# Attention with a cache and a parallel MLP, decode: the first load of wq is cut into 16 and 112 rows

## The chip, the cores and the metric

The kernel runs on one core of a Trainium2 chip. The metric is the device time of one execution in microseconds; a kernel's time is the median over its runs. The core has a matrix engine (TensorE, PE in the profile), a vector engine (VectorE, DVE), an activation engine (ScalarE, ACT), a general engine (GpSimd, POOL) and an engine that only issues DMAs and waits (SyncE, SP). 16 DMA engines move data from HBM, the chip's main memory, to SBUF, the on-chip memory of 128 partitions. "PEq", "SPq" and the like in the profile are an engine's sequencer: the instructions that issue, wait and branch.

## The reference

One token passes through a layer norm, and then through attention over a cache and an MLP at the same time; both are added to the input. All is float32.

```python
# D = 512, 32 query heads, 8 key heads, Sk = 65536 cached keys, Dh = 128, Dff = 1792
q = (x @ wq).reshape(B, Sq, Hq, Dh).transpose(0, 2, 1, 3)
scores = einsum("bhqd,bhkd->bhqk", q, repeat(k_cache, 4)) * Dh ** -0.5
o = einsum("bhqk,bhkd->bhqd", softmax(scores), repeat(v_cache, 4))
A = o.reshape(B, Sq, Hq * Dh) @ wo
B = maximum(x @ w1, 0) @ w2
# with xn = layernorm(x):
return x + A(xn, k_cache, v_cache, wq, wo) + B(xn, w1, w2)
```

## The kernel before

The keys and values of all 8 heads are one row of 524,288 positions, taken in 32 chunks of 16,384 (four to a head). A chunk of k fills the tile `kt`, a chunk of v the tile `vt`, each 128 partitions x 16,384 floats, 8.4 MB. `kt` holds wq ahead of the first chunk and wo behind the last; `wt` holds w1 first and w2 at the end.

**Loads.** All big loads are issued by SyncE, in the order in which they are written. The first, line 151, loads the first 4096 columns of wq for all 128 partitions, a row of 16 KB each. It stands ahead of the hand-synchronised section that begins at line 156. Between them SyncE passes a branch, at which the engines meet. In the section follow the other two parts of wq (line 159; `WQ_CUTS` has 4096, 4096 and 8192 columns), w1 (line 160), and then, each behind a wait, k (line 162) and the loop over v and k (lines 163 to 167). A wait for "kfree" or "vfree" holds an issue until the tile's last reader has signalled. A load adds 16 to its semaphore when all of it has landed. The input x is loaded by ScalarE (lines 234 and 235) on its own queue.

**From x to q.** ScalarE, PE, VectorE and GpSimd compute the layer norm. GpSimd's last step is `xn`, line 212. Then it waits for the first part of wq, which counts on the semaphore "ends" (`take` waits for a count and subtracts it), and copies `xn` into `qpad`, line 214, which signals "q". PE waits for "q", and for the second part of wq on "k", and runs 32 matmuls over all of wq (line 313), of which rounds 0 and 1 read the first part, 2 and 3 the second and 4 to 7 the third. VectorE transposes the results (line 366) and holds rounds 4 to 7 back until the third part has landed on "wq2" (`gates` at line 368). Its last transposes signal "kfree", upon which SyncE issues the first chunk of k.

**GpSimd behind that** waits for w1 and does the MLP's first product (lines 217 to 226); PE's part of it runs in passes beside the attention.

**A turn of the loop.** PE computes the scores of a chunk from `kt`, VectorE transposes them and takes their maximum, ScalarE takes the exponentials, PE multiplies them with `vt`, and VectorE adds to the running result. SyncE issues the next k when VectorE and ScalarE are done with `tr` and `kt`, and the next v when PE is done with `vt`.

Of the kernel before, what the change touches and what calls it, by code (L numbers as in the profile page):

```python
# [40 lines left out]
WQ_CUTS = [4096, 4096, 8192]  # L41
WQ_SEMS = ["ends", "k", "wq2"]
# [2 lines left out]
W2_SUM = 12  # L45
W2_ROWS = 10
PASSES = 3


def take(e, sem, n=1):  # L50

    return e.sem_inc(sem, -n).wait_op(sem, n, "sem-ge")  # L52
# [7 lines left out]
def attention_and_mlp_kernel(  # L60
# [12 lines left out]
    sp, pe, dve, act, pool = nc.sync, nc.tensor, nc.vector, nc.scalar, nc.gpsimd  # L73
    scale = float(DH) ** -0.5

    def sbuf(name, *shape):
        return nc.alloc_sbuf_tensor(name, list(shape), F32).ap()
# [3 lines left out]
    def sem(name):  # L81
        if name not in sems:
            sems[name] = nc.alloc_semaphore(name)
        return sems[name]

    def after(ins, name, n=1):

        return ins.wait_op(sem(name), n, "sem-ge")

    kt = sbuf("kt", P, CHUNK)  # L90
# [47 lines left out]
    wq_row = wq[0].rearrange("p a n -> p (a n)")  # L138
# [9 lines left out]

    load = sp.dma_start(kt[:, : WQ_CUTS[0]], wq_row[:, : WQ_CUTS[0]]).then_inc(sem(WQ_SEMS[0]), 16)  # L151
    tc.no_tile_sem_insts.add(load.ins.name)
    tc.add_to_no_dep_group("first", load.ins)
    tc.declare_fence(pool.nop().ins, group="first")
    section = ctx.enter_context(ExitStack())
    inside = section.enter_context(tc.tile_critical(sync_engine=mybir.EngineType.Pool, no_gpsimd_drain=True))  # L156
    for i in range(1, len(WQ_CUTS)):
        cut = slice(wq_at[i], wq_at[i + 1])
        sp.dma_start(kt[:, cut], wq_row[:, cut]).then_inc(sem(WQ_SEMS[i]), 16)  # L159
# [24 lines left out]
    def link(ins):  # L184

        if chain[0]:
            after(ins, "pool", chain[0])
        chain[0] += 1
        return ins.then_inc(sem("pool"), 1)
# [20 lines left out]
    link(pool.tensor_scalar(st[:, 6:7], st[:, 6:7], -0.5, 1.5, op0=ALU.mult, op1=ALU.add))  # L210
    link(pool.tensor_mul(st[:, 7:8], st[:, 5:6], st[:, 6:7]))
    link(pool.tensor_scalar_mul(xn, xc, st[:, 7:8]))
    take(pool, sem("ends"), 16)
    after(pool.tensor_copy(qpad[:, :XA], xn), "pool", chain[0]).then_inc(sem("q"), 1)
    f = DFF_ALL
    w1_of = [wt[:, a * f : (a + 1) * f] for a in range(XA)]
# [54 lines left out]
    with nc.body("turns", valid_engines=[pe.engine]):  # L271
# [3 lines left out]
        with pe.If(t > 1):  # L275
            after(pe.transpose(pma[:GROUP, :P], m, ident), "d2p").then_inc(sem("p2d"), 1)  # L276
            after(pe.matmul(pmb[:, :GROUP], ones[:GROUP, :], dg, start=True, stop=True), "d2p", 2).then_inc(sem("p2d"), 1)  # L277

            with pe.Fori(0, PASSES):
                for c in range(CT):  # L280
# [175 lines left out]
```

## Time and profile before

| What | Value |
|---|---|
| median of 3 runs | 1303.14 us (1303.03 to 1303.14) |
| span of the profiled execution | 1301.3 us |
| HBM read | 560.99 MB |
| mean rate over the span | 431 GB/s |
| PE busy | 774.9 us (60%) |
| mean granted PE clock | 0.755 |

The span runs from the first to the last instruction of one profiled execution, and the times in its rows count from its start. The median is of whole executions and contains 1.8 us more. Rows of DMAs have a queue's name, the tile loaded and its source. A timeline's row holds the start, the time taken, the engine, the line, the operation, and in brackets the idle time before it with what ended that. "DMA to landing" is the time from issue until the load's semaphore has its count.

### The profile page before, as it was taken

The page shows a single profiled execution, that of the slowest core. Times are in us where ns is not written, and L with a number is a line of the kernel's source. Part 1 is how long each engine was busy: PE and PEld are TensorE (multiplying, and loading weights), DVE is VectorE, ACT ScalarE, POOL GpSimd, SP SyncE. Part 2 cuts the span into 40 slices and gives each one's busy share as a digit, 9 for nine tenths or more (in the row PEclk, how much of TensorE's full clock was granted, in tenths as well). Part 3 has the DMA queues.
Part 4 walks back from the last instruction along what each step waited for, and adds up shares of the span by engine and source line. Part 5 has one row for each costly group of instructions (what it writes and reads, how often), then busy time and mean ns, then how long its engine had stood idle before and what let it go on. Part 6 is the DMA issues. An engine that isn't in the chain of part 4 may idle for free.

```text
span 1301.3 us, 13055 instructions
## 1 busy us (share of the span) xinstructions
PE 774.9 (60%) x5474; PEld 231.1 (18%) x5474; DVE 274.8 (21%) x466; ACT 76.2 (6%) x299; POOL 34.8 (3%) x30
## 2 busy tenths in 40 slices
PE   3365674665576456566555566666567466557557
PEld 1111121111121111121111121111112111112112
DVE  2211222211222220222220122221122221122222
ACT  1000000000000000000000000000000000000000
POOL 1900000000000000000000000000000000000000
PEclk9677877776887777786776777677777777777779
DMA  9999999999999999999999999999999999999998
GB/s 403 451 419 451 419 451 419 435 435 419 451 419 451 419 451 419 449 421 423 447 419 451 419 451 419 451 419 435 435 419 451 419 451 419 451 419 443 427 420 370
DMA packets 11236, 561.02 MB, mean 431 GB/s; under 512 B 1505, under 2 KB 1505, under 8 KB 1890
## 3 DMA queue, kind: packets, MB, share of 16 engines
q1 hardware_dynamic: 11088, 561.00, 99.7%
q10 hardware_dynamic: 146, 0.00, 0.0%
q8 instruction: 1, 0.02, 0.0%
q14 instruction: 1, 0.01, 0.0%
HBM read 560.99 MB, written 0.00 MB: 431 GB/s over the span
## 4 chain that ended last, share of the span: by engine, by line
issue 94%; DMA 3%; POOL 2%; SPq 0%; PE 0%; DVE 0%; POOLq 0%
DMA wt<-w 3%; POOL wt L219 1%; POOL wt L224 0%; POOL wt L222 0%; POOL wt L223 0%; SPq L177 0%; SPq L159 0%; PE banks L339 0%; DVE ysb L417 0%; SPq L151 0%; POOL hT L226 0%; SPq L452 0%; POOLq L156 0%
## 5 line engine op out<-in xcount | busy, mean ns | idle before, releaser
L313 PE MATMUL banks<-kt,qpad 128*32 128x512 f32 x2176 | 310.0, 733 | 311.1 <-PEq L52 308.7
L292 PE MATMUL banks<-vt,probs 128*16 128x512 f32 x2048 | 271.3, 690 | 82.1 <-PEq L52 82.1
L366 DVE STREAM_TRANSPOSE tr<-banks 128x1024 f32<-128x1024 f32 x136 | 170.0, 1250 | 471.4 <-PE banks L313 466.8
L313 PEld LDWEIGHTS banks<-kt,qpad 128*32 128x32 f32 x2176 | 84.5, 131 | 509.6 <-issue 496.3
L281 PE MATMUL banks<-wt,ones 128*1 128x448 f32 x768 | 121.3, 786 | 0.0
L292 PEld LDWEIGHTS banks<-vt,probs 128*16 128x16 f32 x2048 | 68.4, 108 | 298.4 <-issue 298.4
L392 DVE COPY o_sb<-banks 128x512 f32<-128x512 f32 x32 | 22.1, 692 | 455.3 <-PE banks L292 455.3
L254 ACT ACTIVATE corr<-diff 128x8 f32<-128x8 f32 x32 | 6.7, 208 | 1179.8 <-ACTq L52 1179.8
L256 ACT ACTIVATE probs<-tr,nb_new 128x128 f32<-128x128 f32 x128 | 65.3, 521 | 0.0
L276 PE MATMUL banks<-ident,m 128*4 128x128 f32 x32 | 9.7, 303 | 78.9 <-DVE m L384 78.9
L302 PE MATMUL banks<-sel,o_sb 128*128 128x4 f32 x256 | 32.8, 252 | 18.7 <-PEq L52 18.7
L302 PEld LDWEIGHTS banks<-sel,o_sb 128*128 128x128 f32 x256 | 31.0, 191 | 20.6 <-issue 20.6
L226 POOL TENSOR_SCALAR hT<-ysum 128x14 f32<-128x14 f32 x1 | 0.3, 257 | 1220.7 <-DVE ysum L404 1220.7
L384 DVE TENSOR_REDUCE m<-tr 128x4 f32<-128x512 f32 x32 | 32.2, 1006 | 2.9
L281 PEld LDWEIGHTS banks<-wt,ones 128*1 128x1 f32 x768 | 20.2, 100 | 58.9 <-issue 58.4
L277 PE MATMUL banks<-dg,ones 4*128 4x4 f32 x64 | 15.4, 309 | 20.0 <-DVE dg L387 20.0
L256 ACT ACTIVATION_READ_ACCUMULATOR probs<-tr,nb_new 128x1 f32 x128 | 24.0, 187 | 0.0
L276 PEld LDWEIGHTS banks<-ident,m 128*4 128x4 f32 x32 | 2.6, 81 | 108.0 <-DVE m L384 108.0
L219 POOL TENSOR_SCALAR wt<-wt,xn 128x1792 f32<-128x1792 f32 x4 | 19.1, 4797 | 16.5 <-DMA wt<-w 16.5
L277 PEld LDWEIGHTS banks<-dg,ones 4*128 4x128 f32 x64 | 12.6, 245 | 27.1 <-DVE dg L387 27.1
L299 PEld LDWEIGHTS banks<-part_sum,ones 128*128 128x128 f32 x64 | 9.5, 188 | 27.2 <-issue 27.2
L395 DVE TENSOR_TENSOR lo_run<-lo_run,banks 128x8 f32<-128x8 f32 x32 | 5.2, 163 | 40.0 <-DVEq L52 40.0
(69 smaller groups left out, 91.1 us busy)
## 6 DMA issues: line engine op xcount, KB each, us to landing
kt<-wq SPq DMA_DIRECT2D x2, 2048.0 KB, 9.3
kt<-wq SPq DMA_DIRECT2D x1, 4096.0 KB, 20.8
kt<-wo SPq DMA_DIRECT2D x1, 4096.0 KB, 15.5
kt<-wo SPq DMA_DIRECT2D x2, 2048.0 KB, 22.2
wt<-w SPq DMA_DIRECT2D x1, 3584.0 KB, 28.9
wt<-w SPq DMA_DIRECT2D x1, 1536.0 KB, 9.5
wt<-w SPq DMA_DIRECT2D x1, 1024.0 KB, 11.7
kt<-k SPq DMA_DIRECT2D x32, 24.1
```

The source lines that it names most:

```text
L219: last = pool.tensor_scalar_mul(w1_of[a], w1_of[a], xn[:, a : a + 1])
L256: last = act.activation(probs[:, :, g], tr[:, :, g], AF.Exp, bias=nb_new[:, g : g + 1], scale=scale, accum_out=part_sum[:, g : g + 1],)
L276: after(pe.transpose(pma[:GROUP, :P], m, ident), "d2p").then_inc(sem("p2d"), 1)
L277: after(pe.matmul(pmb[:, :GROUP], ones[:GROUP, :], dg, start=True, stop=True), "d2p", 2).then_inc(sem("p2d"), 1)
L281: ins = pe.matmul(hrow[32 * c : 32 * c + 1, :], ones[:, :1], hb[:, :, 32 * c : 32 * c + 32], start=True, stop=True,)
L292: last = pe.matmul(acc[c : c + WIDE * GROUP, :], probs[:, b : b + WIDE, :].rearrange("p b g -> p (b g)"), vt[:, b * DH : (b + WIDE) * DH], ...
L299: pe.matmul(lo_new[:, 0, :], ones, part_sum, start=True, stop=True).then_inc(sem("vfree"), 1)
L302: last = pe.matmul(lo_new[:, 1, :], o_sb[:, b, :], sel[:, b, :], start=(b == 0), stop=(b == WIDE - 1),)
L313: last = pe.matmul(pair[s // 2 % 2][32 * c : 32 * c + 32, s % 2 * 512 : s % 2 * 512 + 512], qpad, kb[:, s * 16 : s * 16 + 16, c, :], start ...
L366: ins = after(dve.transpose(tr2[:, s * 1024 : (s + 1) * 1024], pair[s % 2]), "p2d", s + 1)
L384: dve.reduce_max(m, tr.rearrange("p b i -> p i b")[:, :GROUP, :], axis=AX.X).then_inc(sem("d2p"), 1)
L392: after(dve.tensor_copy(o_sb.rearrange("p b d -> p (b d)"), acc), "p2d", 7).then_inc(sem("d2p"), 1)
```

## The change

The first load is cut by partitions. The load that stays at the place of the old one has the partitions 0 to 15 (`FIRST`), one row of 16 KB for each of 16 DMA engines. The other 112 rows are a second load, the first thing that SyncE issues in the section. Both count on "ends", and GpSimd waits there for 32 rather than 16. Line numbers behind the edits grow by one, and by two behind the second load.

```diff
+FIRST = 16
...
-    load = sp.dma_start(kt[:, : WQ_CUTS[0]], wq_row[:, : WQ_CUTS[0]]).then_inc(sem(WQ_SEMS[0]), 16)
+    load = sp.dma_start(kt[:FIRST, : WQ_CUTS[0]], wq_row[:FIRST, : WQ_CUTS[0]]).then_inc(sem(WQ_SEMS[0]), 16)
     tc.no_tile_sem_insts.add(load.ins.name)
     tc.add_to_no_dep_group("first", load.ins)
     tc.declare_fence(pool.nop().ins, group="first")
     section = ctx.enter_context(ExitStack())
     inside = section.enter_context(tc.tile_critical(sync_engine=mybir.EngineType.Pool, no_gpsimd_drain=True))
+    sp.dma_start(kt[FIRST:, : WQ_CUTS[0]], wq_row[FIRST:, : WQ_CUTS[0]]).then_inc(sem(WQ_SEMS[0]), 16)
     for i in range(1, len(WQ_CUTS)):
         cut = slice(wq_at[i], wq_at[i + 1])
         sp.dma_start(kt[:, cut], wq_row[:, cut]).then_inc(sem(WQ_SEMS[i]), 16)
...
-    take(pool, sem("ends"), 16)
+    take(pool, sem("ends"), 32)
     after(pool.tensor_copy(qpad[:, :XA], xn), "pool", chain[0]).then_inc(sem("q"), 1)
```

On SyncE, at the program's start, the order before is this (`kt<-wq` is the load of wq, the numbers behind it are partitions x floats; `wt<-w` is w1):

```order
L452 UNCONDITIONAL_BRANCH
L151 DMA kt<-wq 128x4096
L452 UNCONDITIONAL_BRANCH
L159 DMA kt<-wq 128x4096
L159 DMA kt<-wq 128x8192
L160 DMA wt<-w 128x7168
L162 DMA kt<-k 128x16384
```

And in the changed kernel:

```order
L454 UNCONDITIONAL_BRANCH
L152 DMA kt<-wq 16x4096
L454 UNCONDITIONAL_BRANCH
L158 DMA kt<-wq 112x4096
L161 DMA kt<-wq 128x4096
L161 DMA kt<-wq 128x8192
L162 DMA wt<-w 128x7168
L164 DMA kt<-k 128x16384
```

One row is new, the load of 112 rows behind the branch. No other engine has another order than before.

## The prediction

> **What bounds the kernel now.** I read the page's queues and slices first, then the run in stretches, then SyncE's issues, then single waits at the start. The page says that one queue's packets fill the 16 DMA engines:
>
> ```profile
> span 1301.3 us, 13055 instructions
> ...
> PE 774.9 (60%) x5474; PEld 231.1 (18%) x5474; DVE 274.8 (21%) x466; ACT 76.2 (6%) x299; POOL 34.8 (3%) x30
> ...
> DMA  9999999999999999999999999999999999999998
> ...
> q1 hardware_dynamic: 11088, 561.00, 99.7%
> ```
>
> No compute engine is over 60%. The stretches (start:end, length, busy time and count per engine, granted clock, mean busy share of the DMA engines, GB/s) say where the rate stands and where it doesn't:
>
> ```profile
> 0.00:1.75 1.75, 0.00 (x0) 0.00 (x0) 0.17 (x1) 0.00 (x0) 0.81 (x9) 1.00 0.00 0
> 1.75:2.40 0.65, 0.00 (x0) 0.00 (x0) 0.29 (x1) 0.44 (x1) 0.49 (x3) 1.00 1.74 403
> 2.40:2.80 0.40, 0.00 (x0) 0.00 (x0) 0.40 (x1) 0.40 (x1) 0.32 (x3) 1.00 0.00 0
> 2.80:3.55 0.75, 0.00 (x0) 0.00 (x0) 0.75 (x1) 0.45 (x1) 0.64 (x5) 1.00 0.90 371
> ...
> 3.50:30.00 26.50, 9.98 (x68) 3.28 (x68) 7.79 (x8) 3.33 (x10) 1.26 (x6) 0.97 1.02 435
> ...
> 70.00:1260.00 1190.00, 722.61 (x5088) 215.58 (x5087) 246.85 (x425) 67.13 (x270) 0.00 (x0) 0.75 1.00 434
> ...
> 1297.00:1301.30 4.30, 1.35 (x38) 0.46 (x28) 0.69 (x2) 0.00 (x0) 0.00 (x0) 1.00 0.09 23
> ```
>
> A packet is put down where it starts, so bytes bunch in short stretches. Nothing moves until 1.75 us. Then 403 GB/s x 0.65 us = 262 KB, which is one row of 16 KB (4096 floats) on each of 16 engines; none starts until 2.80, when the second rows do. From 3.5 us the rate is 435 GB/s and it is still 434 over the 1190 us in the middle: 27.2 GB/s an engine, so a 16 KB row takes 16,384 B / 27.2 GB/s = **0.60 us**. 561 MB at 434 GB/s are 1293 us; with 1.75 us ahead and 4.3 us behind that is 1299 of the 1301.3. The time is one stream, and what shifts its slowest engine shifts the end, as long as loads stay queued. They do:
>
> ```profile
> 0.73 0.39 SPq L151 DMA_DIRECT2D kt<-wq  x1
> 1.34 0.83 SPq L159 DMA_DIRECT2D kt<-wq  x2
> 2.22 0.69 SPq L160 DMA_DIRECT2D wt<-w  x1
> 26.46 0.33 SPq L162 DMA_DIRECT2D kt<-k  x1
> 27.18 0.34 SPq L165 DMA_DIRECT2D vt<-v  x1
> 65.47 0.34 SPq L167 DMA_DIRECT2D kt<-k  x1
> ...
> kt<-wq SPq DMA_DIRECT2D x1, 4096.0 KB, 20.8
> wt<-w SPq DMA_DIRECT2D x1, 3584.0 KB, 28.9
> xT<-x ACTq DMA_DIRECT2D x1, 2.0 KB, 8.2
> ...
> vt<-v SPq DMA_DIRECT2D x1, 42.6
> ```
>
> Columns of the last four: KB and us from issue to landing. The third wq load, issued at about 1.7, lands at 22.5. w1 lands at 2.22 + 28.9 = 31.1 us and the first k load is issued at 26.5, 4.6 us ahead; the first v lands at 27.18 + 42.6 = 69.8 and the second k is issued at 65.5, 4.3 us ahead.
>
> **The change part by part.** It cuts the first DMA (128 rows of 16 KB, 8 to an engine) into 16 rows, issued where the whole was, and 112 rows, issued behind SyncE's branch, ahead of the other wq loads. GpSimd waits for 32 on "ends" in place of 16. Bytes, matmuls and the rest of every engine's order stay.
>
> *One more issue on SyncE.* The L151 row has 0.39 us for one, so the other two wq loads and w1 are issued about 0.4 us later. Their rows are not due until the engines have moved the first 2 MB, 8 x 0.60 = 4.8 us after 1.75; w1's not until all 8.4 MB of wq have gone. Cost 0; without that cover, 0.4 us.
>
> *GpSimd's wait for both parts.* The rows around it:
>
> ```profile
> DMA to landing us min/median/max: 7.2/7.2/7.2
> ...
> 14.15 0.31 POOL L212 TENSOR_SCALAR xn<-xc,st 128x4 f32<-128x4 f32 x1
> 14.52 0.19 POOL L214 COPY qpad<-xn 128x4 f32<-128x4 f32 x1
> ...
> 15.00 5.17 PE L313 MATMUL banks<-kt,qpad 128*32 128x512 f32 x32 [3.03 <-PEq L52]
> ...
> 22.63 3.64 PE L313 MATMUL banks<-kt,qpad 128*32 128x512 f32 x32 [2.46 <-DVEq L368]
> ```
>
> The first row is line 151's: the load lands at 0.73 + 7.2 = 7.9 us. The copy behind the wait starts 0.06 us after the multiply ahead of it, at 14.5, so the wait has 6.5 us to spare. Queued behind it on GpSimd are that copy, which gives PE its q, and then w1's multiplies. Cost 0. If the parts came 6.5 us late or more, q would be late by the rest, but only a lateness beyond 20.2 - 22.6 (the end of PE's first half against the start of its second, which waits for the third wq load through VectorE) would reach the k load.
>
> *An earlier start.* In the stretch 1.75 to 2.40 the 16 first rows start; fine cuts of it put the last start in this one:
>
> ```profile
> 2.28:2.32 0.04, 0.00 (x0) 0.00 (x0) 0.04 (x1) 0.04 (x1) 0.00 (x0) 1.00 0.95 410
> ```
>
> That is 0.04 us x 410 GB/s = one row, 0.55 us behind the first. If a load with an eighth of the rows lets all engines start at 1.75, the slowest gains up to 0.55 us. The second load is issued at 1.34 at the earliest (SyncE's branch ends then), so by the first load's own delays (1.75 - 0.73 = 1.02 to 2.30 - 0.73 = 1.57) its rows are there from 2.36 to 2.91 us, while engines are through with row one from 2.80. The price of its lateness is therefore 0 to 0.1 us now, and all that an earlier first row gains beyond this is waited away again. I take a gain of 0.3, with 0 and 0.55 as ends.
>
> *Rows no longer spread evenly.* Every large load before has 128 rows, so the trace shows 27.2 GB/s on each of 16 lanes, but not what a lane is: an engine, or the group of eight partitions that the engine writes. As long as an engine has partitions of its own the two read alike. Now 16 engines write partitions 0 to 15 together, and then seven rows each of partitions 16 to 127. If a lane is an engine, this costs 0. If a lane is a group of partitions, the first load uses few: with groups that interleave row by row it would use all 16 (cost 0), with blocks of eight neighbours two, so a row takes 8 x 0.60 = 4.8 us; with groups made from runs of four, four lanes, 4 x 0.60 = 2.4 us. I take runs of four, between the ends. Behind it stand 112 rows: the four lanes have 4 rows left, the other twelve all 8, at least 8 x 0.60 = 4.8 us. Together 2.4 + 4.8 = 7.2 us against 4.8 for the load in one: **+2.4 us** with the lanes in perfect use. They won't be: an engine's seven rows run across lane borders, so it queues behind a neighbour in one place and leaves a lane idle in another. I put this at two rows of 0.60, **+1.2 us**, with 0 and four rows (2.4) as ends.
>
> [...]
>
> *Sum:* +2.4 + 1.2 - 0.3 = **+3.3 us** on the slowest engine. It isn't absorbed: k's first issue follows the third wq load (through the second PE half at 22.63) and slides with it, w1's landing slides too, and the 4.6 and 4.3 us of queued work ahead are larger than any unevenness between engines that I allow (four rows, 2.4). Against its own execution: 1301.3 + 3.3 = 1304.6. The median, 1303.14, lies 1.8 us above the span, and I add the same to it: **1306.4 us**. Behind it x also lands later: its 8 packets an engine take turns with wq's rows (issued at 0.98, 8.2 us to landing), so 9.2 becomes 11 to 13 us and the q copy up to 18; PE's first half would end near 24, still ahead of the third wq load at 22.5 + 3.3.
>
> **The rivals.** *Lanes are engines.* Then a row takes 0.60 us wherever it goes and the change is at most a start earlier by 0.55 and at least one late by 0.5 (the new issue's 0.39 and the 0.1): 1302.6 to 1303.6, likeliest 1302.9, not slower. For it speaks that rate and row time are the same for every load; against it that no row in the trace has engines meeting on partitions. It decides if the first rows still take about 1.1 us and the second rows start by 3.5 us.
>
> *Only the first load is hurt.* The seven rows each find free lanes, since early engines pull ahead of late ones and their places spread out: (4 - 1) x 0.60 = +1.8, less 0.3: 1304.6.
>
> *Rows dealt out in turn.* If the second load gives 16 neighbouring rows at a time to the 16 engines, each of its seven rounds is like the first load, 2.4 us: 8 x 2.4 = 19.2 against 4.8, +14.4: 1317.5. The 2 MB would land near 21 us, past the q copy, and k's issue would slide by about as much. Against it: one would have to write seven rounds so, while a block of seven rows per engine is the simpler cut.
>
> *More than 2.6 us faster* asks for more than there is: 1.75 us of empty start, 1.02 of them behind the first issue, and 0.45 us that the first row takes beyond 0.60.
>
> **How the numbers follow.** Lanes by partitions in blocks of seven, 1306.4, own range 1305.8 to 1309.0 (the second term between 0.6 and 2.4, or two lanes in the first load in part): 0.57. Rows in turn: 0.10. Only the first load: 0.11. Lanes are engines: 0.20. Anything faster by more than 0.2%: 0.02. 0.2% is 2.6 us, about what a measurement of this kernel can tell from no change; so slower has 0.57 + 0.10 = 0.67, the same 0.11 + 0.20 = 0.31, faster 0.02. The range from 1302.8 to 1309.0 takes in the forecast, the third case and most of the fourth and leaves the 0.10 at 1317.5 and the lowest part of the fourth.
>
> **What would show it.** In the stretches: first rows that start between 1.75 and 2.0, second rows that start near 4.5 rather than 2.8, and a rate under 435 GB/s up to about 11 us; 435 again from there. k's first issue near 30 in place of 26.46, the last w2 load's end later by as much as that of w1. Wrong, if the second rows start by 3.5 us, if the rate is at 435 by then, or if k's issue slides but the end does not (then the stream has slack that I don't see).

## The result and the profile after

| What | Before | Changed |
|---|---|---|
| median | 1303.14 us (1303.03 to 1303.83, 5 runs) | 1308.79 us (1306.90 to 1312.48, 5 runs) |
| ratio of the means | | 1.0045 (1.0032 to 1.0057) |
| span of the profiled execution | 1301.3 us | 1306.3 us |

The change costs 5.65 us, 0.43%: slower, as forecast, by 1.7 times the +3.3 us of the sum. 1308.79 lies 2.4 us above the forecast of 1306.4 and just inside its range. The runs of the changed kernel also lie 5.6 us apart, those of the kernel before 0.8 us. The page of the changed kernel reads as before but for one instruction and 16 packets more and a longer span; PE is at 59% rather than 60%:

```profile
span 1306.3 us, 13056 instructions
...
q1 hardware_dynamic: 11104, 561.00, 99.7%
```

No average on it shows where 5 us went. The stretches of the changed kernel do (columns as in the prediction: the last three are granted clock, DMA share, GB/s):

```profile
1.75:2.40 0.65, 0.00 (x0) 0.00 (x0) 0.29 (x1) 0.44 (x1) 0.49 (x3) 1.00 1.91 403
2.40:2.80 0.40, 0.00 (x0) 0.00 (x0) 0.40 (x1) 0.40 (x1) 0.32 (x3) 1.00 0.32 42
2.80:3.55 0.75, 0.00 (x0) 0.00 (x0) 0.75 (x1) 0.45 (x1) 0.65 (x5) 1.00 1.89 267
3.55:11.50 7.95, 1.17 (x4) 1.00 (x4) 2.20 (x2) 3.33 (x10) 1.08 (x5) 1.00 0.92 268
11.50:30.00 18.50, 9.76 (x52) 2.51 (x56) 2.59 (x3) 0.00 (x0) 0.19 (x1) 0.86 1.02 437
...
70.00:1260.00 1190.00, 713.62 (x5052) 213.88 (x5052) 242.89 (x422) 68.00 (x274) 0.00 (x0) 0.75 1.00 434
```

And the kernel before in the fourth stretch:

```profile
3.55:11.50 7.95, 0.70 (x3) 0.61 (x3) 2.04 (x1) 1.06 (x6) 0.00 (x0) 1.00 1.01 427
```

The engines count as busy for 92% of that stretch and move 268 GB/s, not 427: they are occupied, but their rows are slow. 159 GB/s less over 7.95 us is 1.26 MB, at 434 GB/s 2.9 us of the stream. From 11.5 us the rate is back. A packet's whole duration is booked where it starts, so the share times the stretch is the mean row where each of 16 engines starts one: 1.91 x 0.65 = 1.24 us for a first row, against 1.74 x 0.65 = 1.13 before. From 2.40 to 3.55 start 42 x 0.40 + 267 x 0.75 = 217 KB, 13 rows, in (0.32 x 0.40 + 1.89 x 0.75) x 16 = 24.7 us of engine time: 1.9 us a row, where one takes 0.60 at full speed. The rows behind the first load suffer more than the first load does.

SyncE's issues in the changed kernel (start, time), and then its loads (KB, us from issue to landing):

```profile
0.73 0.40 SPq L152 DMA_DIRECT2D kt<-wq  x1
1.36 0.32 SPq L158 DMA_DIRECT2D kt<-wq  x1
1.73 0.91 SPq L161 DMA_DIRECT2D kt<-wq  x2
2.69 0.43 SPq L162 DMA_DIRECT2D wt<-w  x1
32.65 0.33 SPq L164 DMA_DIRECT2D kt<-k  x1
```

```profile
kt<-wq SPq DMA_DIRECT2D x1, 4096.0 KB, 23.9
wt<-w SPq DMA_DIRECT2D x1, 3584.0 KB, 31.9
kt<-wq SPq DMA_DIRECT2D x1, 2048.0 KB, 14.7
kt<-wq SPq DMA_DIRECT2D x1, 1792.0 KB, 10.2
kt<-wq SPq DMA_DIRECT2D x1, 256.0 KB, 4.1
xT<-x ACTq DMA_DIRECT2D x1, 2.0 KB, 4.1
```

The first part of wq is complete at 1.36 + 10.2 = 11.6 us rather than 7.9, w1 at 2.69 + 31.9 = 34.6 rather than 31.1: **+3.5 us**; whether that stays to the end is read from further traces below. k's first issue slid further, from 26.46 to 32.65, **+6.2 us**. PE's two halves of the product for q say why:

```profile
16.54 5.96 PE L315 MATMUL banks<-kt,qpad 128*32 128x512 f32 x32 [8.16 <-PEq L53]
26.20 6.25 PE L315 MATMUL banks<-kt,qpad 128*32 128x512 f32 x32 [3.70 <-DVEq L370]
```

The second half starts 3.6 us later, with the third wq load. But it takes 6.25 us rather than 3.64, behind an idle gap of 3.70 us rather than 2.46. Before, w1 landed 4.6 us after k's issue; here 34.6 - 32.65 leaves 1.9 us.

### The profile page after: what moved, and what is told of

It is laid out like the page before. It is cut to its first block, busy times and chain, and to the rows that moved or that the text cites. A ratio compares the mean times of both kernels' runs of the same rounds, so it can differ in the third digit from the quotient of the medians.

```text
span 1306.3 us, 13056 instructions
## 1 busy us (share of the span) xinstructions
PE 772.7 (59%) x5474; PEld 231.0 (18%) x5474; DVE 274.6 (21%) x466; ACT 76.3 (6%) x299; POOL 34.9 (3%) x30
## 4 chain that ended last, share of the span: by engine, by line
issue 93%; DMA 4%; POOL 2%; SPq 0%; PE 0%; DVE 0%; POOLq 0%
DMA wt<-w 4%; POOL wt L221 1%; POOL wt L226 0%; POOL wt L224 0%; POOL wt L225 0%; PE banks L341 0%; SPq L161 0%; SPq L179 0%; DVE ysb L419 0%; SPq L152 0%; PE banks L354 0%; SPq L158 0%; POOL hT L228 0%; SPq L454 0%; POOLq L157 0%
## 5 line engine op out<-in xcount | busy, mean ns | idle before, releaser
L283 PE MATMUL banks<-wt,ones 128*1 128x448 f32 x768 | 117.7, 765 | 0.0
L386 DVE TENSOR_REDUCE m<-tr 128x4 f32<-128x512 f32 x32 | 32.2, 1005 | 2.9
L279 PEld LDWEIGHTS banks<-dg,ones 4*128 4x128 f32 x64 | 11.8, 229 | 27.2 <-DVE dg L389 27.2
L301 PEld LDWEIGHTS banks<-part_sum,ones 128*128 128x128 f32 x64 | 9.5, 188 | 27.2 <-issue 27.2
## 6 DMA issues: line engine op xcount, KB each, us to landing
wt<-w SPq DMA_DIRECT2D x1, 3584.0 KB, 31.9
kt<-wq SPq DMA_DIRECT2D x1, 1792.0 KB, 10.2
```

Source lines behind the costliest of these rows:

```text
L283: ins = pe.matmul(hrow[32 * c : 32 * c + 1, :], ones[:, :1], hb[:, :, 32 * c : 32 * c + 32], start=True, stop=True,)
L301: pe.matmul(lo_new[:, 0, :], ones, part_sum, start=True, stop=True).then_inc(sem("vfree"), 1)
L386: dve.reduce_max(m, tr.rearrange("p b i -> p i b")[:, :GROUP, :], axis=AX.X).then_inc(sem("d2p"), 1)
```

## The experiments

Shortened diffs are against the changed kernel unless said otherwise. "Stream" below is the order of loads that keeps the DMA engines busy; how late it is at a point is read from w1's landing (31.1 us before) and from the issue of y's store (1298.92 us before). A kernel's time is the median of its runs. In the expectations, theory 'late k' is that k's first issue comes so late that the DMA engines run out of queued work.

**Are the lanes engines, or groups of partitions?** Four kernels load the first part of wq in eight loads of 16 rows each. All have the same bytes in the same number of loads; what differs is which 16 partitions are written and which 16 rows of HBM are read. In e6 and e7 the rows of wq stand in another order in the tile, so that their result is not the reference's; the work is the same.

```diff
+    rows = [(slice(16 * i, 16 * i + 16), slice(16 * i, 16 * i + 16)) for i in range(8)]  # e4
+    rows = [(slice(i, P, 8), slice(i, P, 8)) for i in range(8)]                          # e5
+    rows = [(slice(16 * i, 16 * i + 16), slice(i, P, 8)) for i in range(8)]              # e6
+    rows = [(slice(i, P, 8), slice(16 * i, 16 * i + 16)) for i in range(8)]              # e7
...
+    for to, of in rows[1:]:
+        sp.dma_start(kt[to, : WQ_CUTS[0]], wq_row[of, : WQ_CUTS[0]]).then_inc(sem(WQ_SEMS[0]), 16)
...
-    take(pool, sem("ends"), 32)
+    take(pool, sem("ends"), 128)
```

> The first part of wq in eight loads of 16 rows, the rows 16i to 16i+15 of the source into the partitions 16i to 16i+15; each load gives every DMA engine one row. Theory 'partitions' (groups of four neighbours share a lane, so 16 neighbours reach four lanes): rows take up to 2.4 us, the part lands between 14 and 21.5 us, before 7.9. Rival 'source' (what is slow is how the engines read neighbouring rows in HBM): slow too.

> The same eight loads, but load i has every eighth row from i on, in the source and in the partitions. Theory 'partitions' with groups of four: 16 partitions of step eight reach eight lanes, two rows to a lane, rows take 1.2 us, the part lands at 10.5 to 12.5 us. Rival 'source': the rows are apart in HBM, so rows take 0.61 us and it lands near 8.5.

> Strided rows of the source into neighbouring partitions; the rows of wq stand in another order in the tile than in the kernel before. Theory 'partitions': as in the blocks to blocks run, within 1 us. Rival 'source': as in the strided to strided run.

> Neighbouring rows of the source into strided partitions; the rows of wq stand in another order in the tile than in the kernel before. Theory 'partitions': as in the strided to strided run, within 1 us. Rival 'source': as in the blocks to blocks run.

The stretch from 4 to 12 us, in the order e4 (neighbouring partitions from neighbouring rows), e5 (every eighth from every eighth), e6 (neighbouring partitions from every eighth row), e7 (every eighth partition from neighbouring rows):

```profile
4.00:12.00 8.00, 1.17 (x4) 1.00 (x4) 1.75 (x2) 3.33 (x10) 1.08 (x5) 1.00 0.95 117
```
```profile
4.00:12.00 8.00, 1.17 (x4) 1.00 (x4) 1.75 (x2) 3.33 (x10) 1.07 (x5) 1.00 1.04 223
```
```profile
4.00:12.00 8.00, 1.17 (x4) 1.00 (x4) 1.75 (x2) 3.33 (x10) 1.08 (x5) 1.00 1.05 127
```
```profile
4.00:12.00 8.00, 1.17 (x4) 1.00 (x4) 1.75 (x2) 3.33 (x10) 1.07 (x5) 1.00 1.02 213
```

The written partitions decide, the rows read do not: 117 and 127 GB/s into 16 neighbours, 223 and 213 into every eighth partition, with the engines 95% to 105% occupied in all four. A row of 16 KB then takes 0.95 x 16 x 16.4 KB / 117 GB/s = 2.1 us in e4 and, worked out in the same way, 1.2 us in e5. At the prediction's 27.2 GB/s a lane, four lanes are 109 GB/s and eight are 218. Times: 1317.0, 1310.3, 1316.1 and 1309.9 us, one run each, beside 1303.1 before. So how long a row takes depends on the partitions that it is written to. That 16 neighbours have about four of 16 lanes and every eighth partition about eight is an estimate from these rates: 117 and 127 GB/s are 4.3 and 4.7 times 27.2, and 223 and 213 are 8.2 and 7.8 times. No trace shows a lane.

**Is it the cut, or its direction?** The same number of loads, but cut by columns: 512 columns of all 128 rows first, the other 3584 behind the branch (against the kernel before).

```diff
+FIRST = 512
-    load = sp.dma_start(kt[:, : WQ_CUTS[0]], wq_row[:, : WQ_CUTS[0]]).then_inc(sem(WQ_SEMS[0]), 16)
+    load = sp.dma_start(kt[:, :FIRST], wq_row[:, :FIRST]).then_inc(sem(WQ_SEMS[0]), 16)
...
+    sp.dma_start(kt[:, FIRST : WQ_CUTS[0]], wq_row[:, FIRST : WQ_CUTS[0]]).then_inc(sem(WQ_SEMS[0]), 16)
...
-    take(pool, sem("ends"), 16)
+    take(pool, sem("ends"), 32)
```

> The first load keeps the 256 KB but takes them as the first 512 columns of all 128 rows; the other 3584 columns are the second load. Theory 'partitions' (a DMA that writes few partitions is slow, whichever engines carry it): as before, 1302.6 to 1303.6, the rate at 435 GB/s from 3.5 us, the third wq load landing within 0.5 us of before's 22.5. Rival 'small first load' (a second issue behind the branch comes too late, or a small load costs by itself): most of the loss stays, 1306 or more, the third wq load landing past 24.5.

> The kernel with the column cut once more, for a second trace: its runs went from 1304.25 to 1310.45 us although in the traced one the DMA stream ended only 0.1 us later than before and 1.6 us were lost behind it, while the store of y waited to be confirmed. If the spread lies at the end, the last row of w2 ends near 1297.6 again and the whole difference is between the store's issue (1299.0) and its landing. If it lies at the start, the first k row begins later than 30.4 us. If it lies in the loop, the 64 KB rows take more than 2.42 us in some stretch.

e1's stretch, its w1, and its last store (SyncE's issue, then KB and us to landing):

```profile
3.55:11.50 7.95, 1.17 (x4) 1.00 (x4) 2.20 (x2) 3.33 (x10) 1.27 (x6) 1.00 1.01 427
```
```profile
1299.03 0.34 SPq L181 DMA_DIRECT2D y<-ysb  x1
```
```profile
wt<-w SPq DMA_DIRECT2D x1, 3584.0 KB, 28.5
...
y<-ysb SPq DMA_DIRECT2D x1, 2.0 KB, 3.1
```

427 GB/s as before, w1 at 2.69 + 28.5 = 31.2, y's store issued 0.11 us after the 1298.92 of before: cut by columns, the stream loses nothing. Yet e1's time is 1305.48 us (1304.25 to 1310.45, 12 runs), ratio 1.0024 (1.0015 to 1.0033). In its trace the 1.7 us all lie behind the stream: the store of y lands after 3.1 us rather than 1.4. The second trace, e8 (1305.47 us), has the slow store too (2.6 us) and y issued 1.3 us late, with w1 at 31.2 again and k issued at 29.50 rather than 28.27. So the direction of the cut is the cause of the 3.5 us, and it isn't the only thing that the second load costs.

**How much is the 16-row load alone?** Two kernels load the small part into `vt`, which nothing reads before v replaces it, and then all 128 rows into `kt`; once as 16 rows (e14), once as 512 columns (e15), both 262 KB more than before.

```diff
-    load = sp.dma_start(kt[:FIRST, : WQ_CUTS[0]], wq_row[:FIRST, : WQ_CUTS[0]]).then_inc(sem(WQ_SEMS[0]), 16)
+    load = sp.dma_start(vt[:FIRST, : WQ_CUTS[0]], wq_row[:FIRST, : WQ_CUTS[0]]).then_inc(sem(WQ_SEMS[0]), 16)  # e14
+    load = sp.dma_start(vt[:, :512], wq_row[:, :512]).then_inc(sem(WQ_SEMS[0]), 16)                            # e15
...
-    sp.dma_start(kt[FIRST:, : WQ_CUTS[0]], wq_row[FIRST:, : WQ_CUTS[0]]).then_inc(sem(WQ_SEMS[0]), 16)
+    sp.dma_start(kt[:, : WQ_CUTS[0]], wq_row[:, : WQ_CUTS[0]]).then_inc(sem(WQ_SEMS[0]), 16)
```

> The first load takes its 16 rows into the tile of v, where nothing reads them, and the second load takes all 128 rows to their place, so 256 KB more are moved (0.6 us). [...]

> The same with 512 columns of all 128 rows set aside: the same 256 KB more, spread over all partitions. Theory 'partitions': only the 0.6 us of the bytes, the third wq load lands 0.4 to 0.8 us later than before.

w1's issue and its time to landing, in e14 and then in e15:

```profile
2.70 0.44 SPq L162 DMA_DIRECT2D wt<-w  x1
```
```profile
wt<-w SPq DMA_DIRECT2D x1, 3584.0 KB, 30.4
```
```profile
2.68 0.45 SPq L162 DMA_DIRECT2D wt<-w  x1
```
```profile
wt<-w SPq DMA_DIRECT2D x1, 3584.0 KB, 29.1
```

w1 lands at 33.1 and 31.8 us, 2.0 and 0.7 later than before. The 0.7 are the bytes, so the shape of the 16-row load costs 1.3 us. Of the change's 3.5 us the other 2.2 then belong to the 112 rows; that is a difference of single traces, and no run has the 112 rows alone. Times: 1305.26 and 1306.34 us, one run each. e15 has the better stream and the worse time: the second half of PE's product took 6.59 us rather than 3.64, k was issued at 30.12, 1.7 us ahead of w1's landing, and its store of y landed after 3.1 us.

**What does a late k cost?** The kernel before, in which SyncE waits for w1 before it issues the first k:

```diff
     take(sp, sem("kfree"))
+    sp.wait_ge(sem("w1"), 16)
     sp.dma_start(kt, k[0, 0]).then_inc(sem("k"), 16)
```

> The kernel before, in which SyncE waits for w1 to have landed before it issues the first k load, so that the engines run dry once. This prices a dry queue: both theories expect 31.1 + 1.0 us to the first packet, a stop of 1.4 us and slow first rows, 1305 to 1306. If the time goes up by less than 1 us, a late first k cannot be the missing part of the loss; if the runs spread over more than 2 us, a late k alone makes the spread.

1305.94 us (1305.75 to 1306.37, 10 runs), ratio 1.0020 (1.0011 to 1.0029). The first k rows start in this stretch; below it, the same of the kernel before:

```profile
32.20:33.20 1.00, 0.00 (x0) 0.00 (x0) 0.00 (x0) 0.00 (x0) 1.00 (x1) 0.50 3.08 1049
```
```profile
30.30:31.00 0.70, 0.00 (x0) 0.00 (x0) 0.00 (x0) 0.00 (x0) 0.00 (x0) 0.50 3.49 1498
```

1049 GB/s x 1.00 us are 16 rows of 64 KB, 3.08 us each; before, 3.49 x 0.70 = 2.44 us each. They start about 1.9 us later and take 0.64 us longer, together the 2.5 us of the time. In e3 the late issue cost its delay and slow first rows besides.

The two traces of the column cut bear this out. w1 lands at 31.2 us in both; e1 issues k 2.9 us ahead of that, e8 1.7, since PE's second half took 5.34 us in one and 6.57 in the other. Their first k rows, e1 and then e8:

```profile
30.00:30.90 0.90, 0.00 (x0) 0.00 (x0) 0.17 (x1) 0.00 (x0) 0.00 (x0) 1.00 2.72 1165
```
```profile
30.30:31.60 1.30, 0.00 (x0) 0.00 (x0) 0.87 (x3) 0.00 (x0) 0.36 (x1) 1.00 2.28 807
```

Both stretches hold 16 rows, of 2.45 us in e1 and 2.96 in e8, and y is issued 0.1 and 1.3 us later than before. As far as two traces can tell, a k issue 1.8 us later than before (e1) cost nothing, and one 3.0 us later (e8) cost about 1.2 us. No single margin decides: in e10 and e17 below, k is issued 3.0 and 2.9 us ahead of w1's landing, and the first rows take about 3 us.

**The changed kernel with k in time.** Two more executions, without an edit:

> The changed kernel once more, for a second trace: its runs have spans from 1305.1 to 1310.7 us. Theory 'late k': the first 2 MB cost 3.2 to 3.5 us again, and what differs is when the first k load is issued (32.65 in the first trace, later in a slower run) and how slow its first rows are. Rival 'elsewhere': the start is as in the first trace, and the difference lies in the loop or at the store of y.

> The changed kernel, unaltered, a third trace. Theory 'uneven engines behind a late k': if its time is above 1309, the first 64 KB rows of the engines start further apart than the 1.06 us of the first trace, and 64 KB rows of more than 2.5 us are found in the loop. If it is near 1307, they start within 1 us and the loop is free of such rows.

In e9 (1308.12 us) the second PE half took 5.26 us, at a granted clock of 0.50 from 28 to 30 us, and k was issued at 32.38; span 1306.3 again. In e18 (1307.03 us) it took 3.64 us, at a granted clock of 1.00. Its PE, SyncE and stretches:

```profile
16.87 5.76 PE L315 MATMUL banks<-kt,qpad 128*32 128x512 f32 x32 [8.49 <-PEq L53]
26.54 3.64 PE L315 MATMUL banks<-kt,qpad 128*32 128x512 f32 x32 [3.91 <-DVEq L370]
```
```profile
30.37 0.33 SPq L164 DMA_DIRECT2D kt<-k  x1
...
1302.63 0.35 SPq L181 DMA_DIRECT2D y<-ysb  x1
```
```profile
26.00:30.30 4.30, 3.64 (x32) 0.96 (x32) 2.50 (x2) 0.00 (x0) 0.00 (x0) 1.00 0.99 427
...
33.75:34.45 0.70, 0.00 (x0) 0.00 (x0) 0.00 (x0) 0.00 (x0) 0.00 (x0) 1.00 3.47 1498
```

And the profiled execution after the change, where PE was granted half the clock and the first k rows were slow:

```profile
24.70:31.50 6.80, 5.30 (x28) 1.36 (x32) 2.50 (x2) 0.00 (x0) 0.00 (x0) 0.50 0.95 409
33.60:34.30 0.70, 0.00 (x0) 0.00 (x0) 0.60 (x2) 0.00 (x0) 0.00 (x0) 1.00 4.17 1404
```

e18 is close to the forecast: k's issue slid by 3.9 us, the first k rows took 3.47 x 0.70 = 2.43 us as before, y was issued 3.7 us late, the span is 4.0 us longer. In the profiled execution after the change, 1404 GB/s x 0.70 us are 15 rows, and they took 4.17 x 0.70 x 16 / 15 = 3.11 us each, 0.7 more; its y is issued at 1303.94, 5.0 us late. e9 is neither. Its first k rows, and the landing of w1 in e9 and in e18:

```profile
34.10:34.80 0.70, 0.00 (x0) 0.00 (x0) 0.17 (x1) 0.00 (x0) 0.00 (x0) 1.00 3.48 1498
```
```profile
wt<-w SPq DMA_DIRECT2D x1, 3584.0 KB, 32.7
```
```profile
wt<-w SPq DMA_DIRECT2D x1, 3584.0 KB, 32.3
```

In e9 the 16 first rows took 3.48 x 0.70 = 2.44 us: k was issued late, at 32.38, and it cost nothing there. But the loads ahead of k cost more. w1 lands at 2.68 + 32.7 = 35.4 us in e9 and at 2.69 + 32.3 = 35.0 in e18, 4.3 and 3.9 us later than before, where the first trace has 3.5. So one kernel's loads cost 3.5 to 4.3 us. From w1's landing to y's issue the first trace lost another 1.5 us, e9 0.9 (y at 1304.10) and e18 none. The slow first rows account for part of the 1.5; what e9 lost there is not from them and stays open.

The length of PE's gap alone does not say how long the second half takes. Behind gaps of 2.46 us before, 2.14 in e3 and 3.91 in e18 it took 3.64 us; behind gaps of 3.70 in the profiled execution after the change, 4.69 in e9 and 2.05 in e17 below it took 6.25, 5.26 and 5.34. After the change the granted clock was 1.00 until 24.6 us, 2.1 us into the gap, and 0.50 from 24.7 to 31.5; in e9 it was still 1.00 at 26 us, 3.8 us into the gap. What sets it no run here shows.

**Keeping PE busy in the gap** was meant to have the second half at 3.64 us at will. Six kernels put unused matmuls between the halves, in the first turn only: 18 or 5 of 384 columns, 18 with 32 weights, 18 of 96 columns; twice in the columns kernel.

```diff
             for s in range(ROUNDS):
+                if s == ROUNDS // 2:
+                    with pe.If(t < 1):
+                        for _ in range(18):  # 5 in e11 and e12
+                            pe.matmul(pmb[:, 128:512], ones, kt[:, :384], start=True, stop=True)
+                            # e13: pmb[:32, 128:512], ones[:, :32], kt[:, :384]
+                            # e16, e17: pmb[:32, 128:224], ones[:, :32], kt[:, :96]
```

> The changed kernel with 18 more matmuls of 128x384 on PE in turn 0, between the rounds that read the first two parts of wq and those that read the third; their results are never used. They keep PE busy while it waits for the third part. Theory 'late k' (of the loss only 3.3 us come from the first 2 MB; the rest, and the wide spread of the runs, comes from the first k load, which is issued only 1 us before the engines run dry, since PE does its second half at half clock): k's first issue at 30.0 instead of 32.65, the first k rows at their full speed, time 1306.2 to 1306.9, all runs within 1 us. Rival 'uneven engines' (the rest is the slowest DMA engine's own lateness): time 1308 to 1309.5 and runs spread over several us as in the changed kernel.

> The changed kernel with 5 unused matmuls (0.66 us each, 3.3 us in all) on PE in turn 0 while it waits for the third part of wq. 18 of them took 11.9 us and made PE itself late; 5 end before that part lands. Theory 'late k': PE's second half runs at full clock (3.7 us instead of 5.3 to 6.3), k's first issue at 29.9 to 30.5 instead of 32.4 to 32.7, its first rows at full speed, median 1306.4 to 1307.4, and the runs within 1.5 us. Rival 'elsewhere': median 1308 to 1309 and spread as in the changed kernel, though k's first issue is earlier.

> The column cut with the same 5 unused matmuls. Its traces show the first k issued at 28.3 and 29.5 (before: 26.46), up to the point where the engines run dry. Theory 'late k': with PE at full clock k's first issue is at 26.5 to 27, the stream is as before, and what is left against before is only the late confirmation of y's store: 1303.0 to 1305.0, no runs above 1306. Rival 'elsewhere': runs up to 1310 remain.

> The changed kernel with 18 unused matmuls on PE in turn 0, as in the first of these runs, but narrow ones (32 weights, 384 columns), about 0.17 us each and 3.1 us in all. Theory 'late k': k's first issue near 30.3, the last 64 KB row ends at 1272.8 as in the run with five matmuls, the tail behind it is 32 to 32.5 us as in the kernel before, and the median is 1306.3 to 1307.3 with runs within 1.5 us. Rival 'elsewhere': 1308 to 1310.

> The changed kernel with 18 unused matmuls of 96 columns, about 0.17 us each (0.65 us x 96/384), 3 us in all, in PE's wait for the third part of wq. Theory 'late k': k's first issue at 30 to 30.6, the first 64 KB rows of the 16 engines start within 0.5 us of each other, the last 64 KB row ends at 1272.5 to 1273.2 (changed kernel 1274.3, before 1269.2), no stop of PE at the end, median 1306.2 to 1307.3 with runs within 1.5 us. Rival 'elsewhere': 1308 to 1310, or the spread of the changed kernel.

> The column cut with the same 18 matmuls. Theory 'late k': the stream is before's (last 64 KB row at 1269.2 to 1269.5) and the runs lie within 1 us; what remains is the confirmation of y's store, so 1303.0 to 1305.2. Rival 'elsewhere': runs up to 1310.

| Kernel | Median and runs, us | What the trace shows |
|---|---|---|
| e2 | 1312.73 (1312.43 to 1313.89) | k issued at 37.90 |
| e13 | 1312.40 (1311.74 to 1313.35) | k issued at 38.45 |
| e11 | 1309.51 (1309.11 to 1309.89) | k at 30.29, a stop of PE at the end |
| e12 (columns) | 1307.84 (1307.49 to 1307.99) | k at 26.59, a stop of PE at the end |
| e16 | 1308.41 (1307.75 to 1312.97) | k at 31.80, an uneven start of k |
| e17 (columns) | 1308.33 (1306.09 to 1310.52) | second half of 5.34 us, k at 29.78 |

e2 and e13 missed: the fillers weren't short. e2's PE:

```profile
22.25 11.88 PE L315 MATMUL banks<-kt,ones 128*128 128x384 f32 x36
34.06 3.64 PE L319 MATMUL banks<-kt,qpad 128*32 128x512 f32 x32
```

18 matmuls (36 records) took 11.88 us, outlasted the gap and held the second half back; e13's narrower weights changed nothing. With the 18 matmuls the stream is later too. In all four kernels that have them (e2, e13, e16, e17) a packet of instructions is loaded between 15 and 30 us, and in the changed kernel and e11 none; e16's:

```profile
q8 instruction: 1, 0.02, 0.4%
```

w1 lands at 36.2, 36.6 and 36.4 us in e2, e13 and e16, and at 32.7 in e17 with the column cut: 1.3 to 1.7 us later than with 5 matmuls (34.9 in e11, 31.2 in e12). That this packet is the cause is not shown, but these four kernels can't tell what k's issue alone is worth.

In e11 the gap was filled: the second half ran in 3.64 us and k was issued at 30.29. But PE stood still near the end:

```profile
1301.15 0.39 PE L345 MATMUL banks<-wt,hT 128*1 128x128 f32 x6
1304.39 1.01 PE L345 MATMUL banks<-wt,hT 128*1 128x128 f32 x10 [2.85 <-issue]
```

The wait is put down to nothing but the issue of instructions, and the kernels without added instructions have none there. Within it, from 1301.54 to 1304.39, a packet of instructions is loaded:

```profile
q8 instruction: 1, 0.02, 2.8%
```

The changed kernel has one near its end as well, behind 1302.6, when PE has its last 16 matmuls and does not stop. So PE may have waited for instructions; that it did is not shown. e11's y store is issued at 1305.88, 7.0 us later than before; without the 2.85 that is +4.1, and the runs spread by 0.8 us only. So with k in time the change would cost some 4 us, as in e18. e12 had such a stop too (3.08 us) and a stream like that of before. e16 did have the second half in 3.64 us, at a granted clock of 1.00, and k issued at 31.80, and still its profiled run was the slowest, 1312.97. Its stretches:

```profile
34.10:34.80 0.70, 0.00 (x0) 0.00 (x0) 0.00 (x0) 0.00 (x0) 0.00 (x0) 0.50 3.25 1404
34.80:36.00 1.20, 0.00 (x0) 0.00 (x0) 0.00 (x0) 0.00 (x0) 0.00 (x0) 0.50 0.18 79
...
150.00:1250.00 1100.00, 667.86 (x4684) 197.71 (x4684) 225.45 (x392) 63.45 (x252) 0.00 (x0) 0.75 1.00 432
```

One engine's first k row starts in the second stretch, well behind the other 15: 79 GB/s x 1.20 us are 95 KB, that row and one of w1's, of 28 KB. So this engine was late before k. The loop then runs at 432 rather than 434 GB/s, 5 us over 1100, and y is issued at 1308.74, 9.8 us late, of which 5.3 are there at w1's landing. e17 missed in another way: in spite of the fillers the second half took 5.34 us, behind a gap of 2.05 us.

**Is it the shared count?** The columns kernel with its second part on a semaphore of its own (against e1).

```diff
-    sp.dma_start(kt[:, FIRST : WQ_CUTS[0]], wq_row[:, FIRST : WQ_CUTS[0]]).then_inc(sem(WQ_SEMS[0]), 16)
+    sp.dma_start(kt[:, FIRST : WQ_CUTS[0]], wq_row[:, FIRST : WQ_CUTS[0]]).then_inc(sem("part2"), 16)
...
-    take(pool, sem("ends"), 32)
+    take(pool, sem("ends"), 16)
+    pool.wait_ge(sem("part2"), 16)
```

> The column cut with the second part counted on a semaphore of its own instead of the one that y's store shares. If sharing the count has to do with the late confirmation of y, the runs are at 1303 to 1303.7 with little spread. If not, they are at 1304 to 1310 as with the shared count.

1307.36 us (1304.51 to 1311.55, 10 runs), ratio 1.0035: the spread stays, so two loads on one count are not its cause. In its trace w1 lands at 2.69 + 29.5 = 32.2 us, 1.1 later than before, so the column cut's stream isn't free in every execution.

No kernel tried beats the one before. The cut by columns at its best (e1, e8, e12) starts the stream without loss, and gains nothing either: w1 lands at 31.2 us, and at 31.1 before.

## Why the prediction was right or wrong

- **What bounds the kernel: right.** The time is one stream, and a delay at its start is still there at the end: in e18, 3.9 us at w1's landing and 3.7 at y's issue. The rate in the middle is 434 GB/s in both kernels.
- **Lanes are groups of partitions: right** as far as the rates of e4 to e7 show: 117 and 127 GB/s into 16 neighbours, 223 and 213 into every eighth partition. This settles the rival "lanes are engines", which would have had rows of 0.60 us in all four; they took 2.1 us in e4 and 1.2 in e5.
- **The first row of 2.4 us: too high.** It took 1.24 us, but the rows behind it took 1.9; why, no trace shows. The 2.4 stood on lanes made from runs of four partitions, which was the author's choice between values: no run shows how a lane is made up, only the rates of e4 to e7. By e14 against e15 the 16-row load costs 1.3 us beyond its bytes, where the sum had 2.4 - 0.60 = 1.8.
- **The 112 rows: too low**, where the sum had 0.6 of bound lanes and 1.2 of crossed borders: 3.5 to 4.3 us less the 1.3 leave 2.2 to 3.0. The rival "only the first load is hurt" falls with it.
- **An earlier start: not borne out.** The gain of 0.3 us rested on the last of the 16 first rows starting earlier than 2.30. It starts by 2.08 us in the first trace, but at 2.3 in e18 and behind 2.4 in e9, and no run has a time that the gain would explain.
- **Sum of the loads: a little low.** +3.3 was forecast; w1's landing has +3.5, +3.9 and +4.3 in three executions, which the prediction took for one. That the sum comes so near is in part luck, since one of its two large terms is too high and the other too low. The one more issue on SyncE cost nothing: the same issue in e1 left the stream as it was.
- **The signs: mixed.** The rate was low up to about 11 us and whole from there, as foreseen. But the second rows were to start near 4.5 us, and a start by 3.5 was to show the prediction wrong; 13 rows start between 2.40 and 3.55, and are slow. The sign was badly chosen: here the rows took long, 1.9 us, and still started early.
- **GpSimd's wait: right in the end.** Its price needs x, and there the prediction had the wrong sign: "x also lands later" was false. x landed 4.1 us after its issue rather than 8.2. Before, 144 of the 146 packets of its queue start between 4.0 and 9.0 us, beside 144 of SyncE's queue; in the changed kernel all 146 start between 2.5 and 4.0, beside 32. Why its packets start so close together there is not shown. The wait for both parts then delayed the copy of q by 0.8 us, and PE's first half started at 16.54 with the second wq load:

```profile
10.56 0.31 POOL L214 TENSOR_SCALAR xn<-xc,st 128x4 f32<-128x4 f32 x1
11.69 0.19 POOL L216 COPY qpad<-xn 128x4 f32<-128x4 f32 x1 [0.82 <-POOLq L53]
```

- **"k's first issue follows the third wq load ... and slides with it": the step that failed.** It was held to slide by 3.3 us, with 4.6 us of queued work ahead to spare. It slid by 6.2, because PE's second half took 6.25 us and not 3.64. The prediction quoted 3.64 us and took it as the matmuls' price; it was the price of that one stretch, at a granted clock of 1.00, and its own rows had 5.17 us for 32 matmuls of the same shape in the first half, from 15.0 to 20.2 us, also at 1.00. After the change the clock was 0.50 for most of the second half. The first half, which used to wait for q and end 2.46 us before the second, now waits for the second wq load and ends 3.70 us before. Of the 4.6 us of queued work 1.9 were left, the first k rows took 3.11 us rather than 2.43, and y was issued 5.0 us late where w1 had been 3.5. In e18, with 3.64 us at a clock of 1.00, k came at 30.37 and y was 3.7 us late. A late k does not cost in every execution: in e9 it slid by 5.9 us, and the first k rows were as fast as before. e1 against e8 prices it at about 1.2 us, e3 at 2.5 for an issue that waits until the stream has ended.
- **One time for all executions: put at nothing, and wrong.** 1308.79 is the middle of runs from 1306.9 to 1312.5. The loads' 3.5 to 4.3 and a late k of about 1.2 us explain times up to 1303.14 + 4.3 + 1.2 = 1308.6. The rest, up to 1312.5, is not explained: e9 lost 0.9 us behind w1's landing with fast k rows, and in e16, 5 us of slow rows of 64 KB in the loop follow an engine that was late already at w1. Why some executions have such engines stays open; that the uneven start causes the slow loop is a correlation only. The three traces are of executions of 1307.03, 1308.07 and 1308.12 us; none is of the slowest.
- **Rows dealt out in turn** was not what the change does. e4 does just that, and its 1317.0 us are near the 1317.5 forecast, but in part by luck: the sum had 14.4 us for the loads, and e4's w1 lands at 5.44 + 37.8 = 43.2, 12.1 us later than before. Its y is issued 12.6 us late, and the store lands after 2.9 us rather than 1.4.

## What to carry to other kernels

If a load has to be cut, cut it so that every part keeps all 128 partitions: by columns, not by rows. Here the cut by columns left the stream as it was in three traces of five, and the cut by rows made it 3.5 to 4.3 us late, on 2 MB that take 4.8 at 0.60 a row. When a delay is said to be passed on one to one, look again at the slack of the next issue on the queue and at everything that sets it, PE's granted clock too: 1.00 in the second half before and 0.50 for most of it after the change. A price from one row of the trace holds for that row: the same 32 matmuls took 3.64 us there and 6.25 here.

## What the hardware showed besides

- Behind a small first load on SyncE's queue, a load on ScalarE's queue landed sooner: x after 4.1 us (16 rows) and 2.9 us (512 columns) rather than 8.2.
- In e3 a queue that was refilled late paid twice: the next rows started about 1 us after the issue (31.26 to 32.20), and the first of them took 3.08 us rather than 2.44.
- The store of y, 2 KB, landed 1.4 us after its issue in the kernel before, 1.4 to 1.7 in the changed one's three traces, 2.6 to 3.1 in every trace of a kernel that loads 512 columns first, and 2.4 to 2.9 in e4 to e7. What makes the difference is open.
- With 5 matmuls added at the start of a program, PE stood still for 2.85 and 3.08 us at its end (e11, e12), while a packet of instructions was loaded; with 18 added it did not.
